# The upper fp16 half of the q and k stacks: from GpSimd and VectorE to one ScalarE instruction

## The chip, the cores and the metric

The kernel runs on one core of a Trainium2 chip. A core has five engines that run side by side, each with its own queue of instructions in a fixed order: TensorE (PE, with its weight loads shown as PEld), VectorE (DVE), ScalarE (ACT), GpSimd (POOL) and SyncE (SP), which here only issues DMAs. An engine waits when its next instruction needs a result that is not there yet, and what is queued behind waits with it. The metric is the device time of one execution in microseconds; the profile gives the span from the first to the last instruction.

## The reference

Four batches, eight heads, 768 steps, head size 40 (`B, H, S, D = 4, 8, 768, 40`). Per head a gated linear recurrence (an mLSTM cell) runs over the steps, and its output, seen as 320 channels, goes through a gated feed-forward layer with a causal convolution of five taps.

```python
m_new  = np.maximum(f_gate[:, :, t] + m, i_gate[:, :, t])
f_stab = np.exp(f_gate[:, :, t] + m - m_new)
i_stab = np.exp(i_gate[:, :, t] - m_new)
C = f_stab[..., None, None] * C + i_stab[..., None, None] * np.einsum('bhd,bhe->bhde', vt, kt)
n = f_stab[..., None] * n + i_stab[..., None] * kt
h_tilde = np.einsum('bhde,bhe->bhd', C, qt)
denom = np.maximum(np.abs(np.einsum('bhd,bhd->bh', n, qt)), 1.0)[..., None]
y[:, :, t] = sigmoid(o_gate[:, :, t]) * h_tilde / denom
...
gate = sigmoid(causal_conv5(x, conv_w))
out  = (gate * (x @ w_val)) @ w_out
```

## The kernel before, in words

The sequence is cut into six blocks of 128 steps, j = 0 to 5, and each block into two chunks of 64. Within a chunk the recurrence is written as matrix products: scores of keys against queries, times decay factors, times values, plus a state that is carried from chunk to chunk. A unit u is one batch of one block (24 of them), a group g is one chunk of a unit (48).

**The stacks.** Scores are to be as exact as fp32, but the matmuls that make them take fp16. So q and k are split into an upper fp16 half (the value times a power of two, rounded) and a lower half (what the rounding left), and stacked along the contraction: 120 rows, three blocks of 40 (`D`). For q (x = 0) the blocks are upper, upper, lower; for k (x = 1) upper, lower, upper. One product of the stacks gives upper times upper, upper times lower and lower times upper. A stack is prepared per block j, index i = 0 to 3 and kind x, 48 times in all, in tile `stk` (two buffers, by i % 2; each holds both kinds):

- `prep_max` (L288, ScalarE): the greatest absolute value of a row, from the loaded `nat`;
- `prep_scale` (L293 to L300, VectorE): the power of two, `scl`, and its correction `cmp`;
- `prep_hi` (L322, GpSimd): the upper half, written into the first block of the stack;
- `prep_lo` (L327, VectorE): the lower half, value times scale minus upper half, and then a copy of the upper half into its second place (L336, VectorE, fp16 to fp16);
- `prep_tr` (L347, issued by SP): a DMA transpose of the stack into `tq` (queries of a block) or `tk` (keys of a unit, three buffers in turn).

An upper half can be written only when the transpose that last read this buffer has landed.

**The recurrence.** Per group: `args` (L357, TensorE) and `expo` (L368, ScalarE) make the decay factors `dm`; `scores` (L384, TensorE) takes `tk` and `tq`; `probs` (L391, VectorE) multiplies them into `pt`; `keyw` (L403, GpSimd) weights the keys; `heads` (L437 and L439, TensorE) makes the unit's output `ph` and the next state `pc`; `state_out` (L419, ScalarE) copies the state from PSUM into `vc`, from which the next group's `heads` reads it. Then `norm` (L448 to L452, VectorE), `norm_o` (L457, GpSimd, the output gate `sg` over the denominator), `gate_o` (L462, VectorE), `x_tr` (L471, TensorE transposes), `x_copy` (L479 to L481, ScalarE) and `x_rest` (L486 VectorE, L487 GpSimd).

**The feed-forward.** Per block: `conv0` (L496, GpSimd) and eight `conv` (L502, VectorE) for two thirds of the channels, `conv3` (L514, TensorE; L515, ScalarE) for the rest, `sigmoid` (L522), `val` (L537, TensorE), `z_mul` (L542, VectorE), `z_hi` (L546, ScalarE), `z_lo` (L551, GpSimd), `outp` (L563, TensorE), `outp_st` (L568, ScalarE) and the output's DMA (L572). The last block does it in two halves of two batches. The sigmoids and the exponentials need different activation tables, which an ACT_TABLE_LOAD changes. The weights' conversion from their 64-bit form (L581 to L595, L613 to L623) is strewn through blocks 0 to 3; its step on ScalarE is an Abs, L594.

**What sets the order.** The table `LAGS` gives each step a due time in units of groups, and the steps are handed over sorted by it. A scheduler then places the instructions of each engine by its own costs, so the order of an engine changes when a neighbour's cost does. Two things are kept as written: SP's queue, that is nearly all DMAs, and the matmuls of `heads`. The start (block 0 and its loads) is a fixed list as well.

Of the kernel before, what the change touches and what calls it, by code (L numbers as in the profile page):

```python
# [13 lines left out]
AF = mybir.ActivationFunctionType  # L14
ALU = mybir.AluOpType
# [73 lines left out]
def tile_mlstm_gated_ffn(  # L89
# [13 lines left out]
    nc = tc.nc  # L103
    B, H, S, D = q.shape
    P = 128
# [12 lines left out]
    NSH = 5  # L118
    RO = 96
    KA = RO + 3 * H  # L120
    R = B
    PB = P // B
    PS = bass.MemoryType.PSUM
# [22 lines left out]
    def turn(name, i):  # L146
        return i % 4 < T[name]
# [13 lines left out]
    gt = sg[:, ng[0] : ng[1]].rearrange("p (c b t) -> p c b t", c=3, b=B)  # L161
    la = cst.tile([KA, 2, NJ, B, P], BF16, name="la")
    ra = cst.tile([KA, H, NJ, L], BF16, name="ra")
    xc = [cst.tile([P, 2, B, P + 4], F32, name=f"xc{i}") for i in range(2)]
# [10 lines left out]
    sct = [cst.tile([P, B], F32, name=f"sct{i}") for i in range(2)]  # L175
    spg = cst.tile([P, PB, R], BF16, name="spg")
    sel_g = cst.tile([P, PB], F32, name="sel_g")
    sel_b = cst.tile([P, B], BF16, name="sel_b")
    scl = [cst.tile([P, 2, B], F32, name=f"scl{i}") for i in range(2)]
    amx = [cst.tile([P, 2, B], F32, name=f"amx{i}") for i in range(2)]  # L180
    stk = [cst.tile([P, 2, H, P], F16, name=f"stk{i}") for i in range(2)]


    def load_qk(j, x, b0, b1):
        ts = slice(j * P, (j + 1) * P)
        if x == 1 or j == 0:
            hs = slice(b0 * H, b1 * H)
            nc.sync.dma_start(nat[j % 2][:, x, hs], (qv, kv)[x][ts, hs])
            return
        dst = nat[j % 2][:, 0].rearrange("p (h r) d -> p h (r d)", r=R)  # L190
        for b in range(b0, b1):
            nc.sync.dma_start(dst[b * PB : (b + 1) * PB], q[b, :, ts].rearrange("h (g r) d -> g h (r d)", r=R))

# [74 lines left out]
    def spread_in(i, dma):  # L268
        js = slice(0, 1) if i == 0 else slice(1, NJ)
        dma(ra[L : L + NGR, :, js], gdg[i].rearrange("x p b h j t -> (x p b) h j t"))  # L270
        for p in range(2):
            dma(
                la[RO:KA, p, js, :, TOK[p] : TOK[p] + L],
                gda[i].rearrange("h x p j b t -> p (h x) j b t")[p],
# [5 lines left out]
    def part(j, x, i):  # L280
        src = nat[j % 2][:, x]
        if x == 0 and j > 0:
            return src.rearrange("p (h r) d -> p h r d", r=R)[:, :, i]
        return src[:, i * H : (i + 1) * H]
# [23 lines left out]
    def scale_mul(j):  # L308
        nc.vector.tensor_mul(
            spg, sel_g[:, :, None].to_broadcast([P, PB, R]), scl[j % 2][:, 0, None, :].to_broadcast([P, PB, R])  # L310
        )
# [4 lines left out]
        nc.vector.tensor_copy(sct[j % 2], pq)  # L316

    def prep_hi(j, i, x):
        o, v, f = stk[i % 2][:, x, :, 0:D], part(j, x, i), scl[j % 2][:, x, i : i + 1]
        if j > 0 and turn("on_act_hi", 2 * i + x):  # L320
            return nc.scalar.activation(o, v, AF.Copy, scale=f)
        return nc.gpsimd.tensor_scalar(o, v, f, 1.0, op0=ALU.mult, op1=ALU.mult)  # L322

    def prep_lo(j, i, x):
        lo, dup = ((2 * D, D), (D, 2 * D))[x]
        t = stk[i % 2][:, x]
        nc.vector.scalar_tensor_tensor(  # L327
            t[:, :, lo : lo + D],
            part(j, x, i),
            scl[j % 2][:, x, i : i + 1],  # L330
            t[:, :, 0:D],
            op0=ALU.mult,
            op1=ALU.subtract,
        )
        put = nc.scalar.copy if j > 0 and turn("on_act_dup", 2 * i + x) else nc.vector.tensor_copy
        return put(t[:, :, dup : dup + D], t[:, :, 0:D])  # L336

    tq_ = {}

# [7 lines left out]
        nc.sync.dma_start_transpose(t, stk[i % 2][:, x].rearrange("p h n -> p (h n)"))  # L347


    K3 = 3 * D  # L350
    dmt, ptt, kwt, psd_, pss_ = {}, {}, {}, {}, {}

    def args(g):
# [315 lines left out]

    tl = sp.tile([KA, 2, B, P], BF16, name="tl")  # L670
    tr = sp.tile([KA, H, L], BF16, name="tr")
    sel = sp.tile([P, 2, B], BF16, name="sel")
# [8 lines left out]
    with tc.manual_schedule():  # L681
# [11 lines left out]
        for x in range(3):  # L693
            fill(sel[L : L + NGR], [[-B, 2], [-1, B]], -2 * B * x)
            fill(oh1[RO:KA], [[-3, H]], -x)
        for p in range(2):
# [133 lines left out]
    for j in range(NJ):  # L830
        t = j * SJ
# [23 lines left out]
    for u in range(NU):  # L855
        t = 2 * u
        j, b = divmod(u, B)
# [15 lines left out]
    for g in range(NG):  # L873
        for nm, fn in (("args", args), ("expo", expo), ("scores", scores), ("probs", probs), ("keyw", keyw),
                       ("state_out", state_out), ("heads", heads)):
            t = g + lag(nm, g // SJ)
# [56 lines left out]
```

## Time and profile before

| | |
|---|---|
| runs | 294.39, 293.15, 294.20 us; median 294.2 |
| span of the profiled execution | 292.4 us; its device time is not listed apart |
| busy: PE / DVE / POOL / ACT | 207.6 / 227.9 / 176.7 / 155.4 us |
| share of the span | 71 / 78 / 60 / 53% |
| DMA: hardware queue of SP | 37.76 MB, 79.0% of 16 engines' span |
| L322, the upper half (GpSimd) | 48 times, 32.9 us, mean 689 ns |
| L327, the lower half (VectorE) | 48 times, 31.7 us, mean 660 ns |
| L336, the second place (VectorE) | 48 times, 21.3 us, mean 445 ns |
| table loads (ScalarE) | 14 of 1283 ns |

How to read the profile's lines: a group of instructions is given as its line, engine and operation, then output <- inputs by the program's tile names with the shape, the count, the busy time and the mean of one, and behind a second bar the engine's idle time just ahead of them with what ended it. A wait reads "engine line <- what it waited for: us in total, times, longest". A timeline row is start, duration, instruction, and in brackets the idle time ahead of it. SPq is the queue of SP.

### The profile page before, as it was taken

The page shows a single profiled execution, that of the slowest core. Times are in us where ns is not written, and L with a number is a line of the kernel's source. Part 1 is how long each engine was busy: PE and PEld are TensorE (multiplying, and loading weights), DVE is VectorE, ACT ScalarE, POOL GpSimd, SP SyncE. Part 2 cuts the span into 40 slices and gives each one's busy share as a digit, 9 for nine tenths or more (in the row PEclk, how much of TensorE's full clock was granted, in tenths as well). Part 3 has the DMA queues.
Part 4 walks back from the last instruction along what each step waited for, and adds up shares of the span by engine and source line. Part 5 has one row for each costly group of instructions (what it writes and reads, how often), then busy time and mean ns, then how long its engine had stood idle before and what let it go on. Part 6 is the DMA issues. An engine that isn't in the chain of part 4 may idle for free.

```text
span 292.4 us, 6704 instructions
## 1 busy us (share of the span) xinstructions
PE 207.6 (71%) x2411; PEld 165.9 (57%) x2411; DVE 227.9 (78%) x526; ACT 155.4 (53%) x354; POOL 176.7 (60%) x276
## 2 busy tenths in 40 slices
PE   0037437526649374798479989876989999999985
PEld 0015325325437263575468666765767877787984
DVE  7999968757588999988999756997539992794950
ACT  4276642373774932578552497822288456346262
POOL 7566426533749844978964655783439762855541
PEclk9999755556855776789759999795799999999999
DMA  7899799999999995399953999975999230011112
GB/s 138 150 148 197 105 204 162 189 153 163 186 174 230 203 143 106 57 190 206 155 85 74 110 214 192 193 67 96 192 225 150 84 83 2 0 45 48 45 47 90
DMA packets 145897, 38.73 MB, mean 132 GB/s; under 512 B 135176, under 2 KB 143752, under 8 KB 145864
## 3 DMA queue, kind: packets, MB, share of 16 engines
q1 hardware_dynamic: 143044, 37.76, 79.0%
q10 hardware_dynamic: 2820, 0.54, 1.3%
q8 instruction: 19, 0.31, 0.5%
q14 instruction: 14, 0.11, 0.1%
HBM read 17.87 MB, written 4.23 MB: 76 GB/s over the span
## 4 chain that ended last, share of the span: by engine, by line
DVE 24%; PE 22%; POOL 14%; DMA 14%; issue 13%; ACT 6%; SPq 5%; ACTq 0%; POOLq 0%; DVEq 0%
DVE sg L502 6%; PE po L563 5%; PE ph L437 5%; PE pf L537 4%; DMA tq<-stk 4%; DMA tk<-stk 3%; DVE stk L327 3%; POOL kw L403 3%; DVE stk L336 3%; DMA sg<-in_o_gate_dram 2%; PE pss L384 2%; PE pg L514 2%; DMA kp<-nat 2%; DVE pt L391 2%; POOL xl L487 2%
## 5 line engine op out<-in xcount | busy, mean ns | idle before, releaser
L437 PE MATMUL ph<-vc,pt 128*64 128x41 f32 (+1 forms) x768 | 69.8, 258 | 28.6 <-ACT vc L419 17.3
L437 PEld LDWEIGHTS ph<-vc,pt 128*64 128x64 f32 (+1 forms) x768 | 61.9, 167 | 41.0 <-ACT vc L419 20.0
L322 POOL TENSOR_SCALAR stk<-nat,scl 128x320 f16<-128x320 f32 x48 | 32.9, 689 | 40.5 <-DMA tk<-stk 17.9
L502 DVE SCALAR_TENSOR_TENSOR sg<-xc,cwt,sg 128x512 f32<-128x512 f32 (+1 forms) x56 | 50.6, 934 | 4.1 <-POOL sg L496 4.0
L439 PE MATMUL pc<-vc,kw 128*40 128x41 f32 (+1 forms) x704 | 51.5, 236 | 3.1 <-POOL kw L403 1.8
L384 PE MATMUL pss<-tq,tk 120*128 120x64 f16 x384 | 35.5, 270 | 21.5 <-DMA tq<-stk 6.4
L439 PEld LDWEIGHTS pc<-vc,kw 128*40 128x40 f32 (+1 forms) x704 | 45.8, 137 | 7.1 <-issue 3.1
L384 PEld LDWEIGHTS <-tk 120*128 120x128 f16 x384 | 28.8, 134 | 34.5 <-issue 19.0
L368 ACT ACTIVATE dm<-psd 128x512 f32<-128x512 f32 x48 | 28.6, 597 | 32.0 <-DVE pt L391 19.9
L403 POOL TENSOR_TENSOR kw<-kp,dm 128x320 f32<-128x320 f32 (+1 forms) x44 | 37.3, 850 | 9.2 <-DMA kp<-nat 3.1
L391 DVE SCALAR_TENSOR_TENSOR pt<-pss,cmp,dm 128x512 f32<-128x512 f32 x48 | 35.6, 741 | 8.0 <-PE ph L437 6.4
L357 PE MATMUL psd<-ra,la 120*128 120x512 bf16 x48 | 23.7, 494 | 23.8 <-DMA la<-gda 18.4
L327 DVE SCALAR_TENSOR_TENSOR stk<-nat,scl,stk 128x320 f16<-128x320 f32 x48 | 31.7, 660 | 10.7 <-POOL stk L322 10.6
L288 ACT ACTIVATE junk<-nat 128x320 bf16<-128x320 f32 x48 | 22.5, 470 | 22.6 <-DMA nat<-in_q_dram 11.6
L457 POOL TENSOR_TENSOR rs<-sg,den 128x320 f32<-128x320 f32 x24 | 19.4, 807 | 22.4 <-DVE den L452 12.0
L419 ACT COPY vc<-pc 40x328 f32<-40x328 f32 x44 | 18.7, 425 | 24.8 <-PE ph L437 17.7
L487 POOL TENSOR_TENSOR xl<-xc,xh 128x256 fp32r<-128x256 f32 x24 | 19.9, 829 | 16.2 <-ACT xc L480 16.0
L542 DVE TENSOR_TENSOR sg<-pf,sg 128x512 f32<-128x512 f32 (+3 forms) x21 | 12.6, 609 | 13.7 <-ACT sg L522 6.5
L551 POOL TENSOR_TENSOR zl<-sg,zh 128x512 fp32r<-128x512 f32 (+1 forms) x14 | 16.1, 1156 | 11.1 <-ACT zh L546 11.0
L336 DVE COPY stk<-stk 128x320 f16<-128x320 f16 x48 | 21.3, 445 | 0.0
L563 PE MATMUL po<-woh,zh 128*128 128x320 f32 x72 | 19.8, 332 | 0.0
L563 PE MATMUL po<-wol,zh 128*128 128x320 f32 x72 | 18.7, 312 | 0.0
(150 smaller groups left out, 443.4 us busy)
## 6 DMA issues: line engine op xcount, KB each, us to landing
nat<-in_q_dram SPq DMA_DIRECT2D x24, 160.0 KB, 4.0
vc<-in_v_dram SPq DMA_DIRECT2D x12, 320.0 KB, 5.6
sg<-in_o_gate_dram SPq DMA_DIRECT2D x6, 640.0 KB, 6.6
out_dram<-ob SPq DMA_DIRECT2D x24, 160.0 KB, 2.4
kp<-nat SPq DMA_DIRECT2D x22, 160.0 KB, 3.5
nat<-in_k_dram SPq DMA_DIRECT2D x10, 320.0 KB, 4.7
nat<-in_k_dram SPq DMA_DIRECT2D x4, 160.0 KB, 3.5
rawv<-in_moe_w_val_dram SPq DMA_DIRECT2D x4, 160.0 KB, 3.2
```

The costliest lines, as they stand in the source:

```text
L322: return nc.gpsimd.tensor_scalar(o, v, f, 1.0, op0=ALU.mult, op1=ALU.mult)
L327: nc.vector.scalar_tensor_tensor(t[:, :, lo : lo + D], part(j, x, i), scl[j % 2][:, x, i : i + 1], t[:, :, 0:D], op0=ALU.mult, op1=ALU.sub ...
L336: return put(t[:, :, dup : dup + D], t[:, :, 0:D])
L368: nc.scalar.activation(dm, psd_[g], AF.Exp)
L384: nc.tensor.matmul(o, tk[h], tq[:, h], start=True, stop=True)
L391: nc.vector.scalar_tensor_tensor(pt, pss_[g], cmp_[j % 2][:, p, b : b + 1], dmt[g], op0=ALU.mult, op1=ALU.mult)
L403: (nc.vector if turn("on_dve_kw", b) else nc.gpsimd).tensor_mul(kw[0:n], kp[0:n, p, b * H : (b + 1) * H], dmt[g][0:n, :, L - 1 : L].to_bro ...
L437: nc.tensor.matmul(pht[u][p * L : (p + 1) * L, h], ptt[g][0:n, h], mv, start=True, stop=True)
L439: nc.tensor.matmul(pc[n0 : n0 + D, h], kwt[g][0:n, h], mv, start=True, stop=True)
L487: (nc.vector if turn("on_dve_xl", b) else nc.gpsimd).tensor_sub(xlb[j % 2][:, :, b], xb[:, :, b, 4:], xhb[j % 2].bitcast(F32)[:, :, b])
L502: nc.vector.scalar_tensor_tensor(o, xc[j % 2][:, c, b0:b1, t : t + P], cwt[:, c, t : t + 1], o, op0=ALU.mult, op1=ALU.add)
L563: nc.tensor.matmul(pf, z, w, start=(i == 0), stop=(i == len(mm) - 1))
```

## The change

From block 1 on (j > 0) the upper half is written by ScalarE, as an ACTIVATE of Copy with the row's scale, and its output is a pattern with one dimension more: the 40 values of a head go to both of their places in the stack, blocks 0 and 1 for q, blocks 0 and 2 for k. The input is read twice (a broadcast dimension). So one instruction writes 640 elements a partition; GpSimd's L322 and VectorE's copy L336 are left for block 0 alone. The lower half is made as before and reads the first place.

```diff
     def prep_hi(j, i, x):
-        o, v, f = stk[i % 2][:, x, :, 0:D], part(j, x, i), scl[j % 2][:, x, i : i + 1]
-        if j > 0 and turn("on_act_hi", 2 * i + x):
-            return nc.scalar.activation(o, v, AF.Copy, scale=f)
-        return nc.gpsimd.tensor_scalar(o, v, f, 1.0, op0=ALU.mult, op1=ALU.mult)
+        t, v, f = stk[i % 2][:, x], part(j, x, i), scl[j % 2][:, x, i : i + 1]
+        if j == 0:
+            return nc.gpsimd.tensor_scalar(t[:, :, 0:D], v, f, 1.0, op0=ALU.mult, op1=ALU.mult)
+        o = t[:, :, 0:K3].rearrange("p h (c d) -> p h c d", d=D)[:, :, 0 : 2 + x : 1 + x]
+        return nc.scalar.activation(o, v[:, :, None, :].to_broadcast([P, H, 2, D]), AF.Copy, scale=f)
 
     def prep_lo(j, i, x):
...
-        nc.vector.scalar_tensor_tensor(
+        r = nc.vector.scalar_tensor_tensor(
...
-        put = nc.scalar.copy if j > 0 and turn("on_act_dup", 2 * i + x) else nc.vector.tensor_copy
-        return put(t[:, :, dup : dup + D], t[:, :, 0:D])
+        return nc.vector.tensor_copy(t[:, :, dup : dup + D], t[:, :, 0:D]) if j == 0 else r
```

(`turn("on_act_hi", ...)` and `turn("on_act_dup", ...)` are never true with the table as it is, so the kernel before uses GpSimd and VectorE throughout. `K3` is 3 * D.) The new ACTIVATE is line 324 of the changed kernel; lines 121 to 320 count one more there than before, so that L288 is L289.

Over the whole program ScalarE gets 40 instructions of L324 and two table loads (16 in place of 14), GpSimd and VectorE lose 40 each. SP's order is the same row for row. Because the scheduler places by cost, the other engines' orders move too. Three places:

ScalarE, where the preparation of block 2 ends and that of block 3 begins (about 105 us in the profile before). `stk_114` and `stk_115` are the two stack buffers, `8x80` is q and `8x2x40` is k, `cm_vo` is the Abs of the last third of the weights, `vc` the state copy. Before:

```order
L368 ACTIVATE dm_1388<-psd_1386 128x512
L419 COPY vc_85<-pc_1284 40x328
L479 CAST xh_614<-px_1412 128x2x128
L480 COPY xc_90<-px_1412 128x2x128
L481 CAST x_92<-px_1412 64x128
L594 ACTIVATE cm_vo<-rawvo 128x320
L368 ACTIVATE dm_1461<-psd_1457 128x512
```

And with the change:

```order
L368 ACTIVATE dm_1373<-psd_1371 128x512
L324 ACTIVATE stk_115<-nat_81,scl_110 128x8x2x40
L324 ACTIVATE stk_114<-nat_82,scl_111 128x8x80
L324 ACTIVATE stk_115<-nat_82,scl_111 128x8x80
L594 ACTIVATE cm_vo<-rawvo 128x320
L419 COPY vc_85<-pc_1270 40x328
L479 CAST xh_610<-px_1397 128x2x128
L480 COPY xc_90<-px_1397 128x2x128
L481 CAST x_92<-px_1397 64x128
L368 ACTIVATE dm_1444<-psd_1441 128x512
```

Three upper halves and the Abs stand ahead of the state copy and the copies of x, which came first before.

ScalarE, at the sigmoid of block 3's feed-forward and the last exponential (about 243 us). `sg` is the tile of the gate, `dm` the decay factors. Before:

```order
L368 ACTIVATE dm_3268<-psd_3244 128x512
L515 COPY sg<-pg_0_3270 64x512
L368 ACTIVATE dm_3337<-psd_3291 128x512
L522 ACT_TABLE_LOAD
L522 ACTIVATE sg<-sg 128x1536
L546 CAST zh<-sg 128x512
```

And with the change:

```order
L368 ACTIVATE dm_3228<-psd_3204 128x512
L515 COPY sg<-pg_0_3230 64x512
L522 ACT_TABLE_LOAD
L522 ACTIVATE sg<-sg 128x1536
L368 ACT_TABLE_LOAD
L368 ACTIVATE dm_3297<-psd_3251 128x512
L546 CAST zh<-sg 128x512
```

The last exponential now comes behind a sigmoid, so the exponential's table is loaded once more, and the sigmoid's once more ahead of the next L522, that of block 4 (at 265 us before).

VectorE, in the convolution of block 1, among the last key stacks of block 3 (about 149 us). Before:

```order
L502 SCALAR_TENSOR_TENSOR sg<-xc_90,cwt,sg 128x512
L295 TENSOR_SCALAR scl_110<-amx_112 128x4
L293 TENSOR_SCALAR amx_112<-amx_112 128x2
L450 TENSOR_TENSOR den_1820<-ph_1699,den_1820 128x8
L327 SCALAR_TENSOR_TENSOR stk_114<-nat_82,scl_111,stk_114 128x8x40
L336 COPY stk_114<-stk_114 128x8x40
L502 SCALAR_TENSOR_TENSOR sg<-xc_90,cwt,sg 128x512
```

And with the change (L329 is the lower half there):

```order
L502 SCALAR_TENSOR_TENSOR sg<-xc_90,cwt,sg 128x512
L295 TENSOR_SCALAR amx_112<-amx_112 128x4
L329 SCALAR_TENSOR_TENSOR stk_114<-nat_82,scl_111,stk_114 128x8x40
L502 SCALAR_TENSOR_TENSOR sg<-xc_90,cwt,sg 128x512 x2
L296 TENSOR_SCALAR scl_110<-amx_112 128x4
L448 TENSOR_SCALAR den_1798<-ph_1677,sct_105 128x8
```

The copy behind the lower half is gone, and the lower half itself stands two convolution steps earlier.

More of the change, by code (lines that the diff above doesn't have):

```diff
@@ L120, in tile_mlstm_gated_ffn @@
     KA = RO + 3 * H
+    K3 = 3 * D
     R = B
@@ L347, in prep_tr @@
         nc.sync.dma_start_transpose(t, stk[i % 2][:, x].rearrange("p h n -> p (h n)"))
-    K3 = 3 * D
     dmt, ptt, kwt, psd_, pss_ = {}, {}, {}, {}, {}
```

## The prediction

> **What bounds the kernel now.** I read the page first, then a table of busy time by stretch, then the SP queue's own waits, and last single rows where a term of the sum needed them. The page gives the span and, in 40 slices of 7.3 us, how full the DMA engines are.
>
> ```profile
> span 292.4 us, 6704 instructions
> ...
> DMA  7899799999999995399953999975999230011112
> ```
>
> The DMA row falls three times from 9 to 3 or 5 before it ends: near 110 to 124, 146 to 161 and 190 to 204 us. I cut the span there. The columns of the table are the stretch, its length, busy us of PE, PEld, DVE, ACT and POOL with their instructions, the granted clock, the DMA share (over 1 when transfers overlap on an engine) and GB/s.
>
> ```profile
> 36.00:106.00 70.00, 38.69 (x513) 30.98 (x513) 54.09 (x143) 37.05 (x95) 39.34 (x66) 0.59 1.17 181
> 106.00:124.00 18.00, 10.42 (x134) 7.73 (x132) 17.74 (x42) 6.87 (x18) 13.33 (x19) 0.77 0.58 97
> 124.00:144.00 20.00, 16.30 (x193) 11.52 (x192) 16.79 (x27) 15.98 (x33) 16.77 (x27) 0.93 1.20 196
> 144.00:162.00 18.00, 14.90 (x179) 12.80 (x179) 17.75 (x48) 6.88 (x21) 10.95 (x14) 0.74 0.59 73
> 162.00:183.00 21.00, 18.51 (x238) 13.45 (x234) 12.99 (x28) 15.01 (x31) 12.15 (x22) 1.00 1.10 184
> 183.00:204.00 21.00, 15.85 (x195) 13.72 (x195) 18.98 (x46) 9.08 (x28) 13.89 (x19) 0.77 0.83 112
> 226.00:293.00 67.00, 61.19 (x576) 52.38 (x572) 43.39 (x83) 31.05 (x70) 35.30 (x47) 1.00 0.16 50
> ```
>
> So the kernel alternates. In 36 to 106, 124 to 144 and 162 to 183 the DMA engines are full (share 1.10 to 1.20). In 106 to 124, 144 to 162 and 183 to 204 VectorE is (17.74 of 18, 17.75 of 18, 18.98 of 21), while ScalarE is 38%, 38% and 43% busy. After 226 it is TensorE, 61.19 of 67. The SP queue, which issues nearly all DMAs in a fixed order, says what it stood still for:
>
> ```profile
> SPq L347 <- DVE stk L336: 30.6, 7, 7.3
> ...
> SPq L204 <- POOL rs L457: 11.4, 3, 6.3
> ```
>
> It waits 30.6 us for the copy on L336, the instruction that the change takes away, because the transposes (L347) read that stack. The load of the output gate (L204) waits up to 6.3 us for the last use of its buffer, and behind it the next flood of transfers begins. So a VectorE-bound stretch that ends sooner starts the next flood sooner.
>
> **The change part by part.** Forty times, in blocks j = 1 to 5, GpSimd's L322 and VectorE's L336 go and one ScalarE ACTIVATE of 640 elements a partition comes. VectorE's L327 (the lower half) stays behind it, and the SP order does not change. These are the durations now, then the least, median and greatest of the three kinds:
>
> ```profile
> L288 ACT ACTIVATE junk<-nat 128x320 bf16<-128x320 f32 x48 | 22.5, 470 | 22.6 <-DMA nat<-in_q_dram 11.6 <-issue 7.1 <-DMA nat<-in_k_dram 2.0
> L525 ACT ACTIVATE sg<-sg 128x1280 f32<-128x1280 f32 x3 | 3.8, 1270 | 2.3 <-DMA sg<-in_o_gate_dram 2.2
> L522 ACT ACT_TABLE_LOAD x4 | 5.1, 1283 | 0.1
> ...
> L322 POOL TENSOR_SCALAR stk<-nat,scl x48: 527/535/1835, 8.2 to 225.4; 128x320 f16<-128x320 f32 x48
> L327 DVE SCALAR_TENSOR_TENSOR stk<-nat,scl,stk x48: 500/547/1575, 9.1 to 226.7; 128x320 f16<-128x320 f32 x48
> L336 DVE COPY stk<-stk x48: 224/237/1324, 9.8 to 228.2; 128x320 f16<-128x320 f16 x48
> ```
>
> *The new ACTIVATE.* 320 elements take 0.470 us and 1280 take 1.270, so 640 take 0.470 + 320 x (0.800 / 960) = 0.737 us; forty are 29.5 us. In the three VectorE-bound stretches it is 16 of them, 11.8 us onto a ScalarE that is busy 22.8 of 57: no cost by volume. Its place in ScalarE's queue is another matter, below.
>
> *The copy.* It counts only where VectorE is the bound. The first four rows are L336's busy time in 36 to 106 and in those stretches, the two sums are L327's (as many instructions) and L322's (16) over the same 57 us.
>
> ```profile
> 36.00:106.00 70.00, 6.47 (x15) 0.59 1.17 181
> 106.00:124.00 18.00, 1.98 (x5) 0.77 0.58 97
> 144.00:162.00 18.00, 2.05 (x6) 0.74 0.59 73
> 183.00:204.00 21.00, 1.94 (x6) 0.77 0.83 112
> sum 57.00, DVE 10.75; mean DVE 3.58
> sum 57.00, POOL 11.53; mean POOL 3.84
> ```
>
> Term one is 1.98 + 2.05 + 1.94 = **-6.0 us**. The other 23 copies lie beside full DMA engines or after 226 and count nothing. In 36 to 106 that cover is the SP queue; if it were gone, 15 copies at their median 0.237 would be worth 3.6 more.
>
> *Less crowding between VectorE and GpSimd.* The same copy takes 0.237 or up to 1.324 us, L322 0.535 or up to 1.835: they hold each other up. With L322 gone, L327's surplus in the stretches, 10.75 - 17 x 0.547 = 1.45 us, can go. Bounds 0 and 1.45; other GpSimd work stays, but L322 is what ran closest to L327, so I take all, **-1.4**. What the conv rows could gain is a rival below.
>
> *Two more table loads.* The exponential of the last group now stands behind the sigmoid of block 3's feed-forward, so the tables change twice more, 1.283 us each. The second load stands just ahead of block 4's sigmoid (265.09 here):
>
> ```profile
> 265.09 1.49 ACT L522 ACTIVATE sg<-sg 128x1536 f32<-128x1536 f32 x1
> 266.62 0.38 ACT L479 CAST xh<-px 128x256 fp32r<-128x256 f32 x1
> 266.88 0.38 ACT L480 COPY xc<-px 128x256 f32<-128x256 f32 x1
> ...
> 267.34 0.75 POOL L487 TENSOR_TENSOR xl<-xc,xh 128x256 fp32r<-128x256 f32 x1 [3.04 <-ACT xc L480]
> ```
>
> GpSimd waits 3.04 us for that copy, and its L487 at 267.34 is on the chain that ends last. **+1.3.** The first of the two loads has the exponential behind it, beside a TensorE that is busy with the output projection: nothing, and 1.3 more if that cover goes.
>
> *ScalarE's queue.* On GpSimd the upper half stood still for the transposes that must have read the buffer:
>
> ```profile
> POOL stk L322 <- DMA tk<-stk: 17.9, 10, 3.9
> ...
> POOL stk L322 <- DMA tq<-stk: 12.9, 8, 2.6
> ```
>
> These waits move to ScalarE, and behind them now stand the state copies (L419) and the exponentials (L368), for which TensorE and VectorE wait. In the first VectorE-bound stretch three upper halves stand ahead of the weights' Abs (L594), a state copy and the copies of x:
>
> ```profile
> 105.81 0.43 ACT L419 COPY vc<-pc 40x328 f32<-40x328 f32 x1
> ...
> 106.30 0.95 POOL L322 TENSOR_SCALAR stk<-nat,scl 128x320 f16<-128x320 f32 x1 [3.90 <-DMA tk<-stk]
> ...
> 112.97 0.59 PE L357 MATMUL psd<-ra,la 120*128 120x512 bf16 x1 [5.03 <-DVE pt L391]
> ```
>
> The buffer is free at 106.30, three upper halves end at 108.5, the Abs (0.5, as L288's 0.470) at 109.0, so the state copy slips by 3.2 us. TensorE then stands 5.03 us for VectorE anyway: hidden, as long as VectorE gains no more than 1.8 us there (term one has 1.98, so 0.2 may show). In the third stretch two upper halves wait for the scale (L295) and come ahead of two output copies, a third upper half, the copies of x, a state copy and the exponential:
>
> ```profile
> 188.75 0.43 ACT L568 COPY ob<-po 128x320 f32<-128x320 f32 x1 [0.96 <-PE po L563]
> ...
> 192.01 0.60 ACT L368 ACTIVATE dm<-psd 128x512 f32<-128x512 f32 x1
> ...
> 191.34 0.69 DVE L295 TENSOR_SCALAR scl<-amx 128x4 int32<-128x4 int32 x1
> ...
> 196.27 0.74 DVE L391 SCALAR_TENSOR_TENSOR pt<-pss,cmp,dm 128x512 f32<-128x512 f32 x1
> ```
>
> From 192.03, three times 0.737 and at most the 3.26 us that lie between the first two rows, the exponential starts by 197.5 and ends by 198.1; VectorE wants it at 196.27. Cost 0 (the scale comes sooner on a relieved VectorE) to 1.8; I take the middle, **+0.9**.
>
> Sum: -6.0 - 1.4 + 1.3 + 0.9 = **-5.2 us**, a span of 287.2. The page has the span alone; the three runs (293.15 to 294.39, median 294.2) lie 1.8 above it at the median, so the time is **289.0**.
>
> [...] The free copy on VectorE is 0.237 us, the second half of the new ACTIVATE 320 x 0.833 = 0.267. [...]
>
> **The rivals.**
>
> *No change.* SP's fixed order and the transfers set the pace, and VectorE's time comes back as a wait for transposes. For it: the full DMA stretches. Against: in the three stretches the share is 0.58, 0.59 and 0.83, 18.6 us of room, and SP itself waits for L336. It gives 294 to 295.5.
>
> *Slower: ScalarE's queue decides.* The two stalls above are not hidden: 3.2 us at 106 and 4.1 at 192 (192.0 to about 196.1, the exponential). 3.2 + 4.1 + 1.3 - 6.0 = +2.6, so **296.8**. It decides once the stalls that TensorE or VectorE feel exceed 6.0 + 1.4 - 1.3 = 6.1 us in sum. For it: 30.8 us of waits move to the engine that feeds the recurrence. Against: the 5.03 us of TensorE above, and the waits in 36 to 106 lie beside full DMA.
>
> *Much faster: GpSimd's grip on VectorE goes.*
>
> ```profile
> 139.37 4.98 DVE L502 SCALAR_TENSOR_TENSOR sg<-xc,cwt,sg 128x512 f32<-128x512 f32 x1 [1.13 <-POOL sg L496]
> 144.70 1.32 DVE L502 SCALAR_TENSOR_TENSOR sg<-xc,cwt,sg 128x512 f32<-128x512 f32 x1
> ```
>
> The same convolution row took 4.98 us beside a GpSimd without a gap, and 1.32 later. If an emptier GpSimd lets it in at once, 3.7 us go there: 285.3. If L322's own surplus (11.53 - 16 x 0.535 = 3.0) was on the chain too: 282.3. Against: the change takes only L322 away, and GpSimd's other work stays there. [...]
>
> **How the numbers follow.** Forecast 0.46, with a range of its own of 285 to 292. No change 0.17, slower 0.23, much faster 0.14. About 0.5%, 1.5 us, is what a measurement of this kernel can tell from no change: 292.7 to 295.7. Faster is forecast and much faster, 0.60; same 0.17; slower 0.23. From 282 (the lock's end) to 297 (ScalarE's queue) about 0.15 is left out.
>
> **What would show it.** Right: L336 at 8 instructions, L324 near 0.74 us, VectorE's busy time down by 18 us or more, the three stretches each about 2 us shorter, 16 table loads. Wrong: waits of L324 for transposes of 20 us or more with L419 or L368 next behind and TensorE idle for them; VectorE idle in these stretches; or stretches as long as before with SP waiting for something new.

## The result, and the profile after

The changed kernel takes **289.77 us** (median of 5 runs, 288.74 to 292.16) against 293.15 for the kernel before (5 runs, 292.60 to 294.39): a ratio of **0.988**, 95% interval 0.9835 to 0.992. It is faster by about 1.2%, and the forecast was 289.0. The experiments below show that the number came out by other terms than those of the prediction's sum. Where ratios and medians differ a little below, it is because the ratios leave disturbed runs out, and the medians don't; the ratios are always against runs of the kernel before on the same chip.

The page of the changed kernel gives the span, the busy time of each engine, and the DMA row. (The profiled execution took 292.16 us, the other four 288.74 to 289.86.)

```profile
span 290.3 us, 6635 instructions
...
PE 207.8 (72%) x2411; PEld 165.1 (57%) x2411; DVE 206.9 (71%) x486; ACT 186.2 (64%) x396; POOL 151.8 (52%) x236
...
DMA  7899599999999996699924999995979620020112
```

VectorE lost 21.0 us (227.9 before), GpSimd 24.9 (176.7), ScalarE gained 30.8 (155.4). The three dips of the DMA row are still there. These are the groups of the stack's instructions, by form:

```profile
L324 ACT ACTIVATE stk<-nat,scl 128x640 f16<-128x640 f32 x40 | 32.3, 824 | 20.4 <-DMA tk<-stk 11.0 <-DMA tq<-stk 6.7 <-DVE scl L296 2.6
L329 DVE SCALAR_TENSOR_TENSOR stk<-nat,scl,stk 128x320 f16<-128x320 f32 x48 | 30.3, 635 | 12.5 <-ACT stk L324 10.7 <-DMA nat<-in_q_dram 1.3 <-POOL stk L322 0.3
L337 DVE COPY stk<-stk 128x320 f16<-128x320 f16 x8 | 3.9, 487 | 0.0
```

The new instruction takes 824 ns, and VectorE stands 10.7 us for it ahead of its lower halves. That is as long as it stood for GpSimd's upper half before the change:

```profile
L327 DVE SCALAR_TENSOR_TENSOR stk<-nat,scl,stk 128x320 f16<-128x320 f32 x48 | 31.7, 660 | 10.7 <-POOL stk L322 10.6
```

In SP's own queue one wait went and another grew. The wait for the copy is down to 9.0 us, from 30.6:

```profile
SPq L205 <- POOL rs L457: 16.4, 3, 7.1
SPq L348 <- DVE stk L337: 9.0, 3, 4.3
```

but the wait of the output-gate load for GpSimd's `rs` rose from 11.4 to 16.4. That load begins each flood, so its three late starts measure the stretches between. Before:

```profile
121.20 0.40 SPq L204 DMA_DIRECT2D sg<-in_o_gate_dram  x1
162.34 0.40 SPq L204 DMA_DIRECT2D sg<-in_o_gate_dram  x1
201.49 0.40 SPq L204 DMA_DIRECT2D sg<-in_o_gate_dram  x1
```

And after:

```profile
118.75 0.40 SPq L205 DMA_DIRECT2D sg<-in_o_gate_dram  x1
159.75 0.40 SPq L205 DMA_DIRECT2D sg<-in_o_gate_dram  x1
198.81 0.40 SPq L205 DMA_DIRECT2D sg<-in_o_gate_dram  x1
```

It is 2.45 us early at the first and only 2.6 and 2.7 at the others: in this profile the first VectorE-bound stretch gave what was forecast, and the second and third gave 0.1 each, though they lost their copies too. From the load to the next are 41.0 and 39.1 us, as before (41.1 and 39.2). In the same cuts as in the prediction, VectorE has room in the first stretch now and is still nearly full in the second and third:

```profile
106.00:124.00 18.00, 14.39 (x176) 10.47 (x172) 14.53 (x32) 12.10 (x26) 12.89 (x17) 0.84 0.76 122
...
144.00:162.00 18.00, 14.97 (x200) 12.70 (x199) 17.41 (x44) 11.23 (x26) 9.48 (x13) 0.91 0.44 62
...
183.00:204.00 21.00, 17.98 (x251) 13.98 (x252) 18.23 (x47) 14.85 (x38) 11.28 (x17) 1.00 1.03 120
```

### The profile page after: what moved, and what is told of

It reads as the page before. It is cut to its first block, busy times and chain, and to the rows that moved or that the text cites. A ratio compares the mean times of both kernels' runs of the same rounds, so it can differ in the third digit from the quotient of the medians.

```text
span 290.3 us, 6635 instructions
## 1 busy us (share of the span) xinstructions
PE 207.8 (72%) x2411; PEld 165.1 (57%) x2411; DVE 206.9 (71%) x486; ACT 186.2 (64%) x396; POOL 151.8 (52%) x236
## 4 chain that ended last, share of the span: by engine, by line
DVE 30%; PE 23%; DMA 17%; ACT 11%; issue 8%; POOL 6%; SPq 3%; ACTq 0%; POOLq 0%; DVEq 0%
DVE sg L502 9%; PE pf L537 7%; DMA sg<-in_o_gate_dram 5%; PE ph L437 4%; DMA tk<-stk 4%; DMA tq<-stk 4%; PE po L563 4%; DVE stk L329 3%; DVE pt L391 3%; ACT stk L324 2%; PE pg L514 2%; ACT sg L522 2%; PE pss L384 2%; SPq L348 2%; DMA nat<-in_k_dram 1%
## 5 line engine op out<-in xcount | busy, mean ns | idle before, releaser
L437 PE MATMUL ph<-vc,pt 128*64 128x41 f32 (+1 forms) x768 | 66.6, 256 | 17.8 <-ACT vc L419 12.0
L437 PEld LDWEIGHTS ph<-vc,pt 128*64 128x64 f32 (+1 forms) x768 | 59.3, 164 | 29.7 <-ACT vc L419 15.0
L384 PE MATMUL pss<-tq,tk 120*128 120x64 f16 x384 | 33.7, 264 | 25.0 <-DMA tk<-stk 7.8
L439 PE MATMUL pc<-vc,kw 128*40 128x41 f32 (+1 forms) x704 | 49.4, 232 | 2.7 <-ACT vc L419 2.6
L439 PEld LDWEIGHTS pc<-vc,kw 128*40 128x40 f32 (+1 forms) x704 | 43.9, 132 | 9.6 <-POOL wvl L623 2.6
L502 DVE SCALAR_TENSOR_TENSOR sg<-xc,cwt,sg 128x512 f32<-128x512 f32 (+1 forms) x56 | 46.3, 856 | 1.8 <-POOL sg L496 1.6
L384 PEld LDWEIGHTS <-tk 120*128 120x128 f16 x384 | 27.5, 131 | 34.1 <-issue 15.1
L391 DVE SCALAR_TENSOR_TENSOR pt<-pss,cmp,dm 128x512 f32<-128x512 f32 x48 | 35.5, 739 | 14.9 <-PE pss L384 8.2
L324 ACT ACTIVATE stk<-nat,scl 128x640 f16<-128x640 f32 x40 | 32.3, 824 | 20.4 <-DMA tk<-stk 11.0
L329 DVE SCALAR_TENSOR_TENSOR stk<-nat,scl,stk 128x320 f16<-128x320 f32 x48 | 30.3, 635 | 12.5 <-ACT stk L324 10.7
L457 POOL TENSOR_TENSOR rs<-sg,den 128x320 f32<-128x320 f32 x24 | 18.5, 770 | 31.5 <-DVE den L452 17.4
L289 ACT ACTIVATE junk<-nat 128x320 bf16<-128x320 f32 x48 | 22.4, 467 | 17.1 <-DMA nat<-in_q_dram 7.5
L487 POOL TENSOR_TENSOR xl<-xc,xh 128x256 fp32r<-128x256 f32 x24 | 21.0, 873 | 17.5 <-ACT xc L480 17.4
L537 PE MATMUL pf<-xh,wvh 128*128 128x512 f32 (+3 forms) x42 | 13.8, 413 | 5.7 <-ACT dm L368 4.2
```

The costliest lines, as they stand in the source:

```text
L324: return nc.scalar.activation(o, v[:, :, None, :].to_broadcast([P, H, 2, D]), AF.Copy, scale=f)
L329: r = nc.vector.scalar_tensor_tensor(t[:, :, lo : lo + D], part(j, x, i), scl[j % 2][:, x, i : i + 1], t[:, :, 0:D], op0=ALU.mult, op1=ALU ...
L384: nc.tensor.matmul(o, tk[h], tq[:, h], start=True, stop=True)
L391: nc.vector.scalar_tensor_tensor(pt, pss_[g], cmp_[j % 2][:, p, b : b + 1], dmt[g], op0=ALU.mult, op1=ALU.mult)
L437: nc.tensor.matmul(pht[u][p * L : (p + 1) * L, h], ptt[g][0:n, h], mv, start=True, stop=True)
L439: nc.tensor.matmul(pc[n0 : n0 + D, h], kwt[g][0:n, h], mv, start=True, stop=True)
```

## The experiments

My theory was the prediction's: VectorE's copies, on SP's path and in three VectorE-bound stretches, are what the change is worth. The main rival was that the emptier GpSimd is. One warning holds for all runs: SP's order is the same in every kernel here, but the scheduler places the other engines' instructions anew for each edit. Only the fourth run changes little beside its own edit. So single stretches of single profiles swing, and the weight lies on the timed runs.

**One: the upper half alone on ScalarE, the copy kept on VectorE.** This takes the 40 instructions off GpSimd and leaves VectorE all its work.

```diff
-        return nc.scalar.activation(o, v[:, :, None, :].to_broadcast([P, H, 2, D]), AF.Copy, scale=f)
+        return nc.scalar.activation(t[:, :, 0:D], v, AF.Copy, scale=f)
...
-        return nc.vector.tensor_copy(t[:, :, dup : dup + D], t[:, :, 0:D]) if j == 0 else r
+        return nc.vector.tensor_copy(t[:, :, dup : dup + D], t[:, :, 0:D])
```

> The changed kernel, but ScalarE writes the upper half to its first place alone (320 elements) and VectorE copies it to the second, as before: GpSimd is relieved of 40 instructions, VectorE of none. Theory (the gain comes from the copies that left VectorE): no gain, 293 to 295 us, with 40 copies of about 0.35 us each in the stretches between the floods and the output-gate load that stood at 118.8 us in the changed kernel back at 120.5 to 122. Rival (the gain comes from the emptier GpSimd, whose hold on VectorE goes): 290 us, the load at 119.

Measured: 286.90 us, ratio 0.981 (0.977 to 0.986). With every copy in place it is no slower than the changed kernel. The first stretch agrees with the theory, since the load stands at 121.66 us, no earlier than before. The time does not: the load is at 159.53 and 195.66 afterwards.

**Two: the copy alone leaves VectorE,** for ScalarE, and GpSimd keeps its upper halves.

```diff
-        return nc.vector.tensor_copy(t[:, :, dup : dup + D], t[:, :, 0:D]) if j == 0 else r
+        return (nc.vector.tensor_copy if j == 0 else nc.scalar.copy)(t[:, :, dup : dup + D], t[:, :, 0:D])
```

> The kernel before, but the copy to the second place is a ScalarE copy from block 1 on: VectorE is relieved of 40 copies, GpSimd keeps its 40 upper halves, the table loads are 14. Theory: the gain of the changed kernel without its two table loads, 288 to 290 us, the output-gate load of the first VectorE-bound stretch at 119 us. Rival (emptier GpSimd): 293 to 294.5 us, the load at 121.

Measured: 291.23 us, ratio 0.993 (0.990 to 0.997). The load is at 118.06 us, 3.1 early, and at 199.50, 2.0 early: won in the first stretch, partly given back. The time lies between the two expectations. The copies are worth 0.7%, 2 us, when they go alone to ScalarE; the GpSimd instructions were worth 1.9%. My theory falls here as the main cause. The 2 us price this move and not VectorE's time alone, since ScalarE stands 20.6 us for GpSimd's upper halves ahead of these copies.

**Three: the changed kernel, and VectorE copies into a tile that nothing reads.**

```diff
-        return nc.vector.tensor_copy(t[:, :, dup : dup + D], t[:, :, 0:D]) if j == 0 else r
+        return nc.vector.tensor_copy(t[:, :, dup : dup + D] if j == 0 else aside, t[:, :, 0:D])
```

> The changed kernel with its double write, and beside it VectorE still does the 40 copies, but into a tile that nothing reads: VectorE's volume is back, while no transpose waits for a copy. The program has 14 table loads. Theory (VectorE's volume in the stretches between the floods counts, about 6 us): 291.5 to 294 us. Rival (what counted was the transposes' wait for the copy, a latency on SP's queue): 288.5 to 289.8 us, no slower than the changed kernel.

Measured: 290.21 us, ratio 0.990 (0.984 to 0.995), between the two expectations. Against the next run, which has 14 table loads as well, it is 2.7 us (0.0093 x 292.45) for 12.9 us more of VectorE (220.7 busy against 207.8). So the 40 copies are worth 2.7 us here, with some 2 us of uncertainty either way, about 0.2 us for a us of VectorE, and not the 6.0 of the prediction.

**Four: the table loads.** The sigmoid of block 3's feed-forward is kept behind the last exponential.

```diff
-    "gate@3": 3.108, "x_copy@3": 5.277, "x_rest@3": 7.777, "conv@3": 7.767, "conv3@3": 10.905, "sig@3": 11.073,
+    "gate@3": 3.108, "x_copy@3": 5.277, "x_rest@3": 7.777, "conv@3": 7.767, "conv3@3": 10.905, "sig@3": 11.8,
...
-        nc.scalar.activation(g, g, AF.Sigmoid)
+        with tc.issue_after(dmi[NG - 1] if j == 3 else last[0]):
+            nc.scalar.activation(g, g, AF.Sigmoid)
```

(`dmi[g]` is the exponential of group g.)

> The changed kernel with one order fixed: the sigmoid of block 3's feed-forward stands behind the last exponential, so there are 14 table loads and none ahead of block 4's sigmoid; the order of SP, of GpSimd and of VectorE is nearly untouched. Theory (the second extra load is on the path to the end): 1.3 us less, 288.5 us. Rival (ScalarE's load is hidden by the projections of TensorE): 289.8 us, no change.

Measured: 286.80 us, ratio 0.980 (0.976 to 0.985), where the changed kernel had 0.988, and 0.986 when it was measured again (run five): 1.7 to 2.2 us less, where 1.3 were forecast. The trace shows where. This is the wait of GpSimd in the changed kernel, 3.04 us before:

```profile
265.15 0.74 POOL L487 TENSOR_TENSOR xl<-xc,xh 128x256 fp32r<-128x256 f32 x1 [4.18 <-ACT xc L480]
```

And the last stretch of this run, from the first of the last output transfers to the end, is 31.98 us, where the changed kernel has 33.18:

```profile
229.09:252.82 23.73, 23.73 (x274) 19.42 (x274) 15.51 (x30) 13.32 (x31) 15.25 (x22) 1.00 0.14 33
252.82:284.80 31.98, 27.49 (x181) 24.45 (x179) 16.69 (x36) 13.97 (x32) 12.79 (x16) 0.99 0.18 63
```

The second load costs 1.2 us, as forecast, and the first nothing: the stretch ahead is 23.73 us here and in the changed kernel's second profile, just below.

**Five: the changed kernel again,** on the chip of the next three, unedited.

> The changed kernel once more, so that it stands on the same chip as the next three and has a second profile. Both theories: 0.985 to 0.991 of the kernel before. Its own profile of the first time held a granted clock of 0.87 from 230 to 257 us, where TensorE is the bound; if that belongs to the execution and not to the kernel, this profile has 1.00 there and a stretch of about 23.7 us in place of 26.8.

Measured: 288.35 us, ratio 0.986 (0.983 to 0.990). The tail in this profile:

```profile
229.39:253.12 23.73, 23.72 (x274) 19.41 (x274) 15.51 (x30) 14.50 (x32) 15.13 (x22) 1.00 0.15 33
253.12:286.30 33.18, 27.76 (x181) 24.46 (x179) 16.55 (x36) 15.22 (x33) 12.68 (x16) 1.00 0.17 61
```

and in the first one:

```profile
230.30:257.12 26.82, 26.81 (x274) 21.87 (x274) 15.50 (x30) 14.59 (x32) 15.18 (x22) 0.87 0.13 29
257.12:290.30 33.18, 27.75 (x181) 24.47 (x179) 16.54 (x36) 15.19 (x33) 12.67 (x16) 0.98 0.17 61
```

The same 274 matmuls take 23.73 us at a granted clock of 1.00 and 26.82 at 0.87. So 3.1 us of the first profile were its clock, and not the change. The second profile's loads of the output gate are these:

```profile
117.81 0.40 SPq L205 DMA_DIRECT2D sg<-in_o_gate_dram  x1
157.83 0.40 SPq L205 DMA_DIRECT2D sg<-in_o_gate_dram  x1
198.60 0.40 SPq L205 DMA_DIRECT2D sg<-in_o_gate_dram  x1
```

They are 3.4, 4.5 and 2.9 us early. The stretches swing between two profiles of one kernel, but in both the three together gave less than 3 us. This profile ends 6.1 us ahead of the kernel before (286.3 against 292.4). So 4.4 us of it came between the third load and the first of the last outputs (198.60 to 253.12 us here, 201.49 to 260.43 before), where the forecast had put nothing, and 1.2 went to the table load behind. In the first half of that stretch, up to about 230 us, the kernel before had a granted clock of 0.89, and this profile 1.00; how much of the 4.4 us is the clock is open.

**Six: the upper half alone, with 14 table loads.** It joins the edits of runs one and four.

> The upper half alone on ScalarE and the copy on VectorE, as in the kernel that took 286.9 us, and the sigmoid of block 3's feed-forward behind the last exponential (14 table loads). New theory (the gain is GpSimd's, whose queue no longer stands for the transposes; the copies on VectorE cost nearly nothing; the two table loads cost 2.8 us in the tail, 34.77 against 31.97): 284 us. Rival (that kernel's 286.9 us were a lucky order of the scheduler): 287 us or more.

Measured: **284.73 us**, ratio 0.975 (0.971 to 0.979), as the new theory had it. Its six runs (283.30 to 286.17) lie below all six of the changed kernel on that chip (286.94 to 289.43). It beats both kernels, and it has every copy that the change had taken away. SP waits for them as long as ever:

```profile
SPq L348 <- DVE stk L337: 28.8, 8, 6.8
```

**Seven: GpSimd's load put back, without its waits.** Beside the kernel of run six GpSimd computes the upper halves into a tile that nothing reads.

```diff
-        return nc.scalar.activation(o, v, AF.Copy, scale=f)
+        nc.gpsimd.tensor_scalar(aside, v, f, 1.0, op0=ALU.mult, op1=ALU.mult); return nc.scalar.activation(o, v, AF.Copy, scale=f)
```

> The kernel of the upper half alone with 14 table loads, and beside it GpSimd still computes the 40 upper halves, into a tile that nothing reads and that waits for no transpose: its volume is back, its waits are not. Theory (the waits for transposes in GpSimd's queue were what cost): within 1 us of the run without it, about 284 to 285 us. Rival (GpSimd's volume, or its crowding of VectorE, was what cost): 3 to 5 us more, 287 to 289 us, and the 128x512 convolution steps back from 0.94 us towards 1.06.

Measured: 290.93 us, ratio 0.994 (0.991 to 0.997). That is 6.2 us more than run six, more even than the rival had, and leaves little of its gain. So the second theory, that it was the waits for transposes in GpSimd's queue, falls as well: the added instructions have none here. What costs is the work on GpSimd itself. The pages of runs six and seven, first six:

```profile
PE 202.8 (72%) x2411; PEld 162.1 (57%) x2411; DVE 216.6 (77%) x526; ACT 173.4 (61%) x394; POOL 151.5 (54%) x236
```

then seven:

```profile
PE 207.4 (72%) x2411; PEld 164.2 (57%) x2411; DVE 222.5 (77%) x526; ACT 174.5 (61%) x394; POOL 177.0 (61%) x276
```

GpSimd has 25.5 us more, and VectorE, with the same 526 instructions, 5.9. Of the 5.8 us between the two profiles, 4.5 lie in the second stretch, from one load of the output gate to the next. First run six, then run seven:

```profile
121.48:158.32 36.84, 30.39 (x423) 23.49 (x422) 31.55 (x73) 27.09 (x63) 24.06 (x32) 0.95 0.94 148
122.43:163.76 41.33, 32.55 (x437) 24.88 (x436) 35.34 (x81) 28.27 (x66) 32.27 (x44) 0.95 0.92 135
```

The granted clock is 0.95 in both, so it does not explain these 4.5 us. It may have a part in the rest: behind the third load run seven has 0.88 from 198.00 to 227.31 us, where run six has 1.00. In the second stretch the extra work stands in front of the weighted keys `kw`, on which the recurrence's next state depends:

```profile
149.85 1.83 POOL L324 TENSOR_SCALAR aside<-nat,scl 128x320 f16<-128x320 f32 x1
151.66 0.72 POOL L487 TENSOR_TENSOR xl<-xc,xh 128x256 fp32r<-128x256 f32 x1
152.37 0.53 POOL L324 TENSOR_SCALAR aside<-nat,scl 128x320 f16<-128x320 f32 x1
152.87 1.19 POOL L403 TENSOR_TENSOR kw<-kp,dm 104x320 f32<-104x320 f32 x1
155.41 3.04 POOL L324 TENSOR_SCALAR aside<-nat,scl 128x320 f16<-128x320 f32 x4 [1.35 <-issue]
158.41 0.73 POOL L403 TENSOR_TENSOR kw<-kp,dm 128x320 f32<-128x320 f32 x1
```

One of them takes 1.83 us where another takes 0.53. So there are two ways in which the load can cost, GpSimd's queue and the crowding with VectorE. The convolution steps did not slow down (mean 925 ns, in run six 962), against what the rival had expected. TensorE's weight loads for the next state (L439) stand 3.4 us for the added instructions. How the 6.2 us divide was not tried apart.

**Eight: ScalarE writes the upper half a second time,** into a tile that nothing reads, beside the kernel of run six.

```diff
-        return nc.scalar.activation(o, v, AF.Copy, scale=f)
+        r = nc.scalar.activation(o, v, AF.Copy, scale=f); nc.scalar.activation(aside, v, AF.Copy, scale=f); return r
```

> The kernel of the upper half alone with 14 table loads, and ScalarE writes it a second time, into a tile that nothing reads: 40 x 0.56 = 22 us more on ScalarE, twice what the double write of the changed kernel adds to a single one (40 x 0.265 = 10.6). Theory that ScalarE's volume is what takes the copies' gain back: 2 to 6 us more, 286 to 290. Rival (ScalarE has room, no cost by volume, as the prediction had it): 284 to 285 us.

Measured: 286.62 us, ratio 0.980 (0.976 to 0.984). 22.3 us more on ScalarE cost 1.9, where 25.8 on GpSimd cost 6.2. By the ratios it is 1.6 us, give or take as much. So ScalarE is clearly the cheaper place, by a factor of about three on these numbers, and whether it is quite free is not shown. VectorE's busy time rose by 2.9 us here too, to 219.5, with GpSimd's as in run six. So of the 5.9 us in run seven not all can be put down to GpSimd.

**Nine: two ScalarE instructions** in place of the double one, in the kernel of run four.

```diff
-        return nc.scalar.activation(o, v[:, :, None, :].to_broadcast([P, H, 2, D]), AF.Copy, scale=f)
+        r = nc.scalar.activation(o[:, :, 0], v, AF.Copy, scale=f); nc.scalar.activation(o[:, :, 1], v, AF.Copy, scale=f); return r
```

> The changed kernel with 14 table loads, but its ScalarE instruction is two: the first place, then the second place, 320 elements each from the same input. VectorE's lower half has to wait for the first alone (0.56 us in place of 0.82), ScalarE spends about 40 x 0.29 = 11.7 us more. Theory (the double write hurts because VectorE stands for it, 11.4 us ahead of the lower halves in the changed kernel and 3.7 with the single write): those waits fall to 4 to 7 us and the time to 284 to 286 us. Rival (ScalarE's volume hurts): 287 to 288.5 us, slower than the 286.8 of the one instruction.

Measured: 289.61 us, ratio 0.983 (0.978 to 0.989), not to be told from the one instruction (0.980). The theory's own sign failed: VectorE stands 13.7 us for the upper halves, not 4 to 7, though it now waits for the first of the two alone (of the pair that runs from 140.08 to 141.08 us, VectorE's lower half starts at 140.66).

```profile
L329 DVE SCALAR_TENSOR_TENSOR stk<-nat,scl,stk 128x320 f16<-128x320 f32 x48 | 31.0, 648 | 14.7 <-ACT stk L324 13.7 <-POOL stk L322 0.3 <-DMA kp<-nat 0.2
```

So the length of the double write is not why VectorE waits.

**Ten: a third stack buffer** in the kernel of run six.

```diff
-    stk = [cst.tile([P, 2, H, P], F16, name=f"stk{i}") for i in range(2)]
+    stk = [cst.tile([P, 2, H, P], F16, name=f"stk{i}") for i in range(3)]
...
-        t, v, f = stk[i % 2][:, x], part(j, x, i), scl[j % 2][:, x, i : i + 1]
+        t, v, f = stk[(4 * j + i) % 3][:, x], part(j, x, i), scl[j % 2][:, x, i : i + 1]
...
-        dm = wk.tile([P, H, L], F32, name=f"dm{g}", tag="dm", bufs=3)
+        dm = wk.tile([P, H, L], F32, name=f"dm{g}", tag="dm", bufs=2)
```

> The kernel of the upper half alone with 14 table loads, and three stack buffers in turn in place of two (for the room, the decay factors have two buffers in place of three, and the junk output of the Abs is of one byte). ScalarE waited 14.7 us ahead of its upper halves for transposes that still read the buffer. Theory that these waits, now in front of the state copies and exponentials, hold the recurrence: 2 to 4 us less, 281 to 283 us. Rival (they lie beside other work): 284 to 285 us, or more by what the missing third buffer of the decay factors costs.

Measured: 298.21 us, ratio 1.016 (1.012 to 1.019), slower than anything else here. ScalarE's upper halves wait longer for the transposes, 21.4 us in place of 14.7, and TensorE for the state copy behind them:

```profile
PEld ph L437 <- ACT vc L419: 21.4, 11, 5.8
```

where the kernel of run six has

```profile
PEld ph L437 <- ACT vc L419: 17.0, 9, 5.5
```

The decay factors lost a buffer in this kernel too, the unread output of the Abs is of one byte, and one small tile moved into the room of another. So it does not say what a third stack buffer is worth. That state copies wait behind upper halves and transposes is argued from these rows; the share of it in the 13 us is open.

**Eleven: the double write on GpSimd.** VectorE is relieved of its copies as in the change, and the work goes to GpSimd.

```diff
-        return nc.scalar.activation(o, v[:, :, None, :].to_broadcast([P, H, 2, D]), AF.Copy, scale=f)
+        return nc.gpsimd.tensor_scalar(o, v[:, :, None, :].to_broadcast([P, H, 2, D]), f, 1.0, op0=ALU.mult, op1=ALU.mult)
```

> The kernel before with the double write on GpSimd: one GpSimd instruction of 640 elements makes the upper half in both places, VectorE loses its 40 copies, ScalarE gets nothing. GpSimd's instruction is taken at 0.535 + 0.3 to 0.5 us, 12 to 20 us more in all. Theory of the prediction (VectorE's copies are worth 6 us): 288 to 290 us as long as GpSimd has room. New theory (a us on GpSimd costs about 6.2 / 25.8 = 0.24 us, a copy on VectorE little): 3 to 5 us more for GpSimd and 1 to 2 less for the copies, 294 to 297 us.

Measured: 294.79 us, ratio 1.005 (1.001 to 1.008). The same copies go as in the change, GpSimd has 14.2 us more than before (176.7), and the kernel becomes slower by half a per cent. At run seven's 6.2 / 25.8 = 0.24 us for a us of GpSimd, the 14.2 us cost 3.4 by estimate; 1.3 were measured, which leaves 2.1 for the copies, as in run two, and not 6.0. The page:

```profile
PE 206.4 (71%) x2411; PEld 163.7 (56%) x2411; DVE 221.9 (76%) x486; ACT 158.0 (54%) x356; POOL 190.9 (65%) x276
```

VectorE has the 486 instructions of the changed kernel and is busy 221.9 us with them, not 205.9 or 206.9 (its two profiles): 15 to 16 us more, beside 39 us more on GpSimd. Against the kernel before it lost 17.4 us of copies and only 6.0 us of its busy time.

**Twelve: half of GpSimd's load.** As run seven, for the 20 key stacks alone (the added call stands behind `x and`).

> The kernel of the upper half alone with 14 table loads, and GpSimd still computes the 20 upper halves of the keys into a tile that nothing reads: half the extra load that cost 6.2 us. If the cost goes with GpSimd's volume: 3 us more than without it, about 287 to 288.5 us. If it came from one place where the full load happened to stand: either as without it, 284 to 285.5, or nearly all of it, 290 us.

Measured: 288.99 us, ratio 0.982 (0.977 to 0.987). By the ratios that is 0.0074 x 293 = 2.2 us over run six for 11.8 us of GpSimd, and 5.7 for 25.8 in run seven, about 0.2 us a us both times. This agrees with a cost that goes with the volume and does not prove it. The 2.2 us are uncertain by 1.9, and the place is another: the stretch that took 41.3 us in run seven, here from 123.12 to 159.67 us, takes 36.6, as in run six. So the 0.2 is an average of this kernel, not a rule.

## Why the prediction came out right, point by point

The time, its sign and its range held, and so did most of the signs to look for: 8 copies left, VectorE 21.0 us down, 16 table loads. But only the first of the three stretches is 2 us shorter, in both profiles, and one of its signs of being wrong showed in part: stretches as long as before in the first profile, with SP waiting longer for `rs`, a wait that is not new. The terms of the sum did not hold either, so that the time came out near the forecast is in good part luck. Some of it lies in where the sum starts: the forecast counted from 294.2, the median of three runs, and from the 293.15 of five its -5.2 would have given 288.0. These are the terms:

| step of the prediction | forecast, us | measured, us |
|---|---|---|
| the copies leave VectorE | -6.0 | -2.0 for ScalarE alone (run two); with the double write in their place +1.7 (runs four and six, 0.980 and 0.975, intervals that overlap) |
| less crowding, as L322 leaves GpSimd | -1.4 | -7.5 for the whole move of the upper half (run six, 0.0255 x 293); 5.7 to 6.2 come back with the load (run seven) |
| two more table loads | +1.3 | +1.2 in the trace, 1.7 to 2.2 in the times (run four) |
| ScalarE's queue | +0.9 | not told apart; 22 us more on ScalarE cost 1.6 to 1.9 (run eight) |
| sum | -5.2 | -3.4, and -4.5 when measured again (run five) |

**The step that failed** is "It counts only where VectorE is the bound", 1.98 + 2.05 + 1.94 us, and the reading of SP's 30.6 us behind it. The wait was real, but it was not the copy's price: the kernel of run six waits 28.8 us for the same copies and is the fastest of all. Most of the time freed on VectorE became idle time. It was idle for 64.5 us before (292.4 - 227.9) and for 83.4 in the changed kernel (290.3 - 206.9). No single wait took it. The one for the upper half, ahead of L329, is as long as before: 10.6 then, 10.7 now (11.4 in the second profile, 3.7 in run six). Others grew, most of all that of `probs` (L391) for the scores, from 1.3 to 8.2 us (5.6 in the second profile). So which result holds VectorE up in place of its own copies is not shown. Why the upper half isn't there sooner stays open too. Run nine excludes the length of the double write. The two buffers and the transposes that still read them are the next candidate (17.7 us of L324's waits), and run ten didn't settle it.

**The term that was far too small** is GpSimd's. I priced L322's leaving by the surplus of one VectorE row in 57 us, 1.45 us. Its 40 instructions were 26 us of an engine that also makes the weighted keys and `rs`, and 25.8 us of the same work, put back without its waits, cost 5.7 to 6.2 us (run seven). The prediction had the mechanism as a rival, "GpSimd's grip on VectorE", at 282 to 285, with 0.14. Its size was nearer the truth than the main forecast's term: the upper half moved alone, with the tables in order, gives 284.7. The mechanism that it names, a convolution step let in sooner, is not shown: those steps took 1064 ns before and 962 in run six, but 925 in run seven with the load back. Nor does any run show the lock that is named with the chances, at 282. What the runs show is that VectorE's 526 instructions take 5.9 us more beside 25.5 us more of GpSimd (run seven), and 2.9 us more in run eight, with GpSimd's work as in run six. The gain did not show in full in the changed kernel's time, because the table loads took part of it back, and by the medians the exchange of the copy for a longer ScalarE instruction did as well.

**The new instruction** was put at 0.737 us and takes 0.824. The two rows that I drew the line through have no scale from a tile, and this one has one per row. The single write of run six, 320 elements with the same kind of scale, takes 0.559, where the Abs (L288) takes 0.470 on 320. From 0.559 to 0.824 the second 320 elements cost 0.265 us, 0.83 ns each, as on the line (0.267). So the 0.087 us by which the estimate fell short lie in the first 320 elements (0.559 - 0.470 = 0.089). That the scale is the reason was not shown.

**ScalarE's queue in the first place** went as worked out. The three upper halves, the Abs and then the state copy, which was forecast to follow at 109.0:

```profile
106.47 2.27 ACT L324 ACTIVATE stk<-nat,scl 128x640 f16<-128x640 f32 x3 [1.52 <-DMA tk<-stk]
108.64 0.47 ACT L594 ACTIVATE cm_vo<-rawvo 128x320 f32<-128x320 f32 x1
109.14 0.43 ACT L419 COPY vc<-pc 40x328 f32<-40x328 f32 x1
```

It cost nothing: the product `pt` that stood at 112.16 us stands at 109.12. In the third place the exponential starts at 192.90 us, where the prediction had it by 197.5 at the latest: the first two upper halves got their scale at 188.97, not 192.03.

**The rivals.** No change is out by the interval. Slower by ScalarE's queue is out for the change. TensorE's wait for the state copy fell from 17.3 us before to 12.0:

```profile
PE ph L437 <- ACT vc L419: 12.0, 6, 5.5
```

One price spoke against the change and counted for nothing in the sum: the free copy takes 0.237 us on VectorE, and the second half of the ScalarE instruction 0.267 by estimate, 0.265 as measured (0.824 less 0.559). Its direction agrees with runs one and six, where the copy on VectorE is at least as good as the second half of the ScalarE instruction (0.981 and 0.975, against 0.988 and 0.980).

## What to carry to other kernels

A queue's long wait for an instruction need not be what that instruction costs (here 28.8 us of waits in the fastest kernel); move it alone, or put it back alone, before it is given a price. When work leaves an engine that shares the chain with the busy one, count its whole volume on that engine, and not only the rows that ran beside it (here 5.7 to 6.2 us for 25.8 us of GpSimd, where 1.4 were forecast). When a change bundles two moves, time each by itself: here the move of the upper half was worth 2.5%, and the changed kernel, with two table loads and the move of the copy beside it, had 1.2 to 1.4% left.

## What the runs showed of the hardware

The changed kernel's two profiles differ by 3.1 us in one stretch, and the granted clock tells why. In the first, TensorE pauses 1.61 us ahead of its scores at 229.41 (they wait for L568), and the clock falls within the next two us; the columns are as before, the clock third from the end:

```profile
228.00:230.00 2.00, 0.59 (x9) 0.54 (x9) 1.05 (x2) 1.07 (x3) 0.72 (x1) 1.00 0.25 90
230.00:232.00 2.00, 1.92 (x21) 1.42 (x18) 1.03 (x2) 1.95 (x7) 0.54 (x1) 0.79 0.75 217
232.00:234.00 2.00, 2.00 (x41) 2.00 (x40) 0.98 (x3) 0.51 (x2) 1.02 (x3) 0.50 0.92 167
...
238.00:240.00 2.00, 2.00 (x17) 1.17 (x15) 0.00 (x0) 0.47 (x1) 0.43 (x3) 1.00 0.00 0
```

In the second the pause at the same place is 1.01 us, and the clock stays:

```profile
228.00:230.00 2.00, 1.43 (x18) 1.03 (x17) 1.24 (x2) 1.92 (x5) 0.00 (x0) 1.00 0.31 111
...
232.00:234.00 2.00, 2.00 (x18) 1.51 (x18) 1.53 (x6) 1.74 (x5) 1.33 (x3) 1.00 0.43 89
```

The 0.79 over two us and the 0.50 over the next six come to 6.8 us at a clock of 0.50, by estimate ((0.21 x 2 + 0.50 x 6) / 0.50). TensorE is the bound there (1.92 to 2.00 us busy of every 2.00), so that is 3.4 us at most, and 3.1 were measured. So a pause that was 0.6 us longer went with 3.1 us more of time, in one execution and not in the other. That the pause is the cause rests on this pair of profiles alone.
